# Held weight loads, idle matmuls in early gaps, and six output transposes moved from DMA to TensorE, under a newly searched order, in a recurrent-attention kernel fused with an MLP

## The chip, the cores and the metric

The kernel runs on one core of a Trainium2 chip. The metric is the time of one execution in device microseconds (us). The span of a profile, from the first to the last instruction, is 1.7 to 1.9 us shorter than that time in the profiled runs. In the profiles PE is TensorE, PEld its weight loads, DVE VectorE, ACT ScalarE, POOL GpSimd, and SP the sync engine, whose queue issues most of the transfers; a transfer has landed when its completion is recorded. An execution counts as slow when it is over 1.5% above the fastest of the same kernel. A change under 2% counts as "the same".

## The reference

The inputs are r, k and v (4 batches, 8 heads, 768 steps, 48 elements a head), w and u (8 heads x 48), and two weight matrices, 384 x 2048 and 2048 x 384.

```python
for t in range(S):                       # recurrent attention, state of 48 x 48 per head
    cur = einsum('bhd,bhe->bhde', u * k[t], v[t])
    y[t] = einsum('bhd,bhde->bhe', r[t], state + cur)
    state = w * state + einsum('bhd,bhe->bhde', k[t], v[t])
x = y as (3072 tokens, 384)
h = x @ w_in
g = where(h >= 1, h, where(h <= -1, 0, (h + 1)**2 / 4))
return g @ w_out
```

## The kernel before

The kernel cuts the 3072 tokens into 24 units of 128 steps, and two units make one block of the MLP. A unit's attention is done in parallel over its 128 steps: R and K are weighed with powers of w (products on POOL and VectorE), turned, multiplied to scores, masked, and multiplied with V; a state is carried from chunk to chunk. The unit's output x is then turned to xT, as layer 1 needs the model dimension on the partitions. In the profiles RKW is the weighed R and K before they are turned and RK after it, AT are the masked scores, Vb is V in bf16, st and T are the state's update and the state, h_p and o_p the results of the two layers, and gT is the activation. No scheduler decides the order: a list of some 1300 words, found by a search, gives the order in which all operations are issued, and each engine executes its own in that order.

```python
PE_T, PE_D, ONE = 8, 6, 2                    # units 0 to 7: turned by TensorE; the others by DMA

def load_u():
    nc.sync.dma_start(out=u_bc, in_=row_bcast(u))          # one row to 128 partitions
def load_wc():                                             # 4-byte gather, twice
    for s in range(2):
        nc.sync.dma_start(out=wc[rows[s], :], in_=w.rearrange("(p s) d -> s d p", s=2)[s])
def load(i, name):                                         # K, R or V of one unit
    nc.sync.dma_start(out=t[name, i], in_=src[b, :, c*C:(c+1)*C, :].rearrange("h s d -> s h d"))
def xp_pe(i):                                              # output turned by TensorE ...
    for kk in range(nKb):
        nc.tensor.transpose(xp[:, kk, :], t["x", i][:, kk*128:(kk+1)*128], ident)
def xp_copy(i):
    copy(("xT", i), xT[i // UB][:, i % UB], t["xp", i])
def xp_dma(i):                                             # ... or by DMA
    nc.sync.dma_start_transpose(xT[i // UB][:, i % UB], t["x", i])
def load_in(q):                                            # one quarter of w_in; w_out likewise
    nc.gpsimd.dma_start(out=w_in_sb[:, :, q*FQ:(q+1)*FQ], in_=w_in_src[:, :, q*FQ:(q+1)*FQ])
# [... weighing, scores, masks, states, layer 1 (h_p), its activation (gT), layer 2 (o_p), stores ...]
```

Of the kernel before, what the change touches and what calls it, by code (L numbers as in the profile page):

```python
# [16 lines left out]
w ld:K:0 u gi:0 ld:R:0 ln tab:K ld:K:1 tab:R Kw:0 ld:V:0 gi:1 ld:V:1 Rw:0 li:0 trp:0 gi:2 trc:0 KU1:0 at:0  # L17
KU2:0 li:1 mk:0:1 gi:3 mk:0:0 dg:0 Vb:0 ld:R:1 VD:0 st:0 Kw:1 y:0 wc x:0 li:3 KU1:1 xs:0 xp:0 Rw:1 xT:0 dec
KU2:1 trp:1 Ta:0:1 L1:0:0:0 ld:K:2 trc:1 Ta:0:0 Vb:1 dg:1 L1:0:1:0 ld:R:2 VD:1 sm:0:0:0 st:1 go:1 sm:0:1:0
Ta:1:1 at:1 li:2 Ta:1:0 L1:0:3:0 Tb:0:1 Kw:2 mk:1:0 Tb:0:0 Tb:1:1 mk:1:1 sm:0:3:0 KU1:2 Tb:1:0 ld:V:2 Rw:2  # L20
y:1 KU2:2 x:1 ld:R:3 xs:1 trp:2 go:0 dg:2 L1:0:2:0 ld:K:3 trc:2 xp:1 Vb:2 ld:V:3 sm:0:2:0 VD:2 go:3 xT:1
at:2 ld:K:4 st:2 mk:2:1 go:2 L1:0:1:1 ld:V:4 Ta:2:0 L1:0:0:1 Rw:3 sm:0:1:1 lo:0 Kw:3 Ta:2:1 Tb:2:0 L1:0:2:1
mk:2:0 sm:0:0:1 KU1:3 Tb:2:1 L1:0:3:1 sm:0:2:1 y:2 Kw:4 ld:R:4 trp:3 x:2 trc:3 KU2:3@DVE ld:R:5 dg:3 KU1:4
xp:2 L2:0:1:0 sm:0:3:1 lo:1 L2:0:0:0 Rw:4 L2:0:0:1 xT:2 L2:0:1:1 Vb:4 xs:2 at:3 KU2:4 L1:1:0:0 mk:3:1 trp:4
ld:K:5 VD:3 sm:1:0:0 L1:1:2:0 mk:3:0 Vb:3 trc:4 ld:V:5 L1:1:1:0 dg:4 sm:1:2:0 st:4 VD:4 ld:R:6 y:3 Kw:5
Ta:4:1 sm:1:1:0 L2:0:1:2 Ta:4:0 at:4 ld:K:6 x:3 st:3 Rw:5 L1:1:3:0 xs:3 KU1:5 mk:4:0 ld:V:6 L2:0:0:2
sm:1:3:0 xp:3 Ta:3:1 L2:0:1:3 KU2:5 xT:3 mk:4:1 lo:2 L2:0:0:3 trp:5 Tb:3:1 Ta:3:0 Td:4 trc:5 dg:5 L1:1:0:1
Vb:5 y:4 VD:5 sm:1:0:1 lo:3 L1:1:2:1 Kw:6 x:4 at:5 Tb:4:1 Rw:6 sm:1:2:1 L1:1:1:1 mk:5:1 xs:4 xp:4 KU1:6
mk:5:0 st:5 L1:1:3:1 ld:R:7 xT:4 Ta:5:0 sm:1:1:1 trp:6 KU2:6 Ta:5:1 ld:K:7 y:5 sm:1:3:1 L2:0:0:4 Td:5 Tb:4:0
dg:6 ld:V:7 L2:0:1:4 x:5 Vb:6 L2:0:0:5 Tb:3:0 L2:0:1:5 trc:6 ld:R:8 L2:0:1:6 xp:5 st:6 Rw:7 L2:0:0:6 Ta:6:1  # L30
xT:5 ld:K:8 L2:0:0:7 Ta:6:0 L2:0:1:7 Tb:5:1 oc:0:0 Kw:7 at:6 Tb:5:0 ld:V:8 xs:5 oc:0:1 L1:2:0 Td:6 mk:6:0
L2:1:0:0 ld:K:9 sm:2:0 L2:1:0:1 KU1:7 mk:6:1 trp:7 ld:R:9 L1:2:2 KU2:7 trc:7 L1:2:4 ld:V:9 Vb:7 sm:2:2 y:6
dg:7 Vb:8 L2:2:1:0 Tb:6:0 x:6 so:0:0 L1:2:1 Kw:8 sm:2:4 so:0:1 at:7 sm:2:1 ld:R:10 L2:1:0:2 Rw:8 mk:7:1
Tb:6:1 st:7 L1:2:3 xs:6 ld:K:11 Ta:7:1 KU1:8 xp:6 Ta:7:0 sm:2:3 L2:1:0:3 mk:7:0 L2:1:0:4 ld:V:10 xT:6 KU2:8
L1:2:5 st:8 L2:1:0:5 sm:2:5 tr:8 Td:7 y:7 dg:8 Kw:9 L2:1:0:6 x:7 Tb:7:0 L2:1:0:7 Tb:7:1 ld:R:11 L1:2:6 Rw:9
L1:2:7 sm:2:6 ld:K:12 Ta:8:1 Vb:9 L2:2:1:1 oc:1:0 sm:2:7 xp:7 KU1:9 ld:K:10 Ta:8:0 L2:2:1:2 xs:7 L2:1:1:0
L2:1:1:1 Td:8 xT:7 ld:V:11 L2:1:1:2 KU2:9 L2:1:1:3 L2:1:1:4 L2:1:1:5 tr:9 L2:1:1:6 Vb:10 dg:9 at:8 Rw:10
L1:3:3 ld:R:12 mk:8:1 L1:3:0 Kw:10 sm:3:3 mk:8:0 ld:V:12 st:9 L2:1:1:7 sm:3:0 Ta:9:1 Rw:11 L2:2:1:3 oc:1:1
L1:3:1 ld:V:13 Ta:9:0 Kw:11 y:8 sm:3:1 so:1:0 L1:3:2 x:8 Tb:8:1 tr:10 Td:9 st:10 L1:3:4 sm:3:2 KU1:11 Tb:8:0
at:9 Ta:10:0 so:1:1 sm:3:4 L2:2:1:4 KU1:10@DVE ld:R:13 L1:3:5 xs:8 mk:9:1 KU2:10 L2:2:1:5 sm:3:5 ld:K:13  # L40
L1:3:6 mk:9:0 Vb:11 L2:2:1:6 Ta:10:1 sm:3:6 xp:8 L1:3:7 KU2:11 dg:10 y:9 sm:3:7 tr:11 L2:2:1:7 Td:10 x:9
st:11 Rw:12 oc:2:1@ACT at:10 Tb:9:0 L2:2:0:0 ld:K:14 Tb:9:1 L2:2:0:1 Kw:12 dg:11 L2:2:0:2 xs:9 L2:2:0:3
ld:R:14 mk:10:0 L2:2:0:4 KU1:12 L2:2:0:5 mk:10:1 L2:2:0:6 xp:9 L2:2:0:7 KU2:12 Ta:11:1 L2:3:1:0 oc:2:0
L2:3:1:1 ld:V:14 y:10 Vb:12 Ta:11:0 L2:3:0:0 x:10 Tb:10:0 Kw:13 L2:3:0:1 so:2:1 Tb:10:1 at:11 tr:12 L2:3:1:2
Vb:13 L2:3:0:2 Rw:13 mk:11:1 L2:3:0:3 xs:10 L2:3:1:3 so:2:0 mk:11:0 L2:3:1:4 ld:K:15 Rw:14 L2:3:0:4 st:12
dg:12 L2:3:0:5 L1:4:0 xp:10 Ta:12:1 Td:11 Ta:12:0 Kw:14 y:11 sm:4:0 ld:R:15 L1:4:1 x:11 Tb:11:1 Td:12 L1:4:2
sm:4:1 ld:V:15 KU1:14 L2:3:1:5 sm:4:2 L1:4:3 tr:13 KU1:13 Tb:11:0 at:12 sm:4:3 L1:4:4 mk:12:0 KU2:13 xs:11
xp:11 L1:4:5 mk:12:1 sm:4:4 KU2:14 L2:3:0:6 ld:K:16 dg:13 sm:4:5 L2:3:1:6 L1:4:6 Vb:15@ACT Vb:14 ld:R:16
dg:14 y:12 Rw:15 sm:4:6 L1:4:7 x:12 ld:V:16 Tb:12:0 L2:3:1:7 Kw:15 sm:4:7 L2:3:0:7 st:13 tr:14 st:14
oc:3:0@ACT oc:3:1 KU1:15 at:13 Tb:12:1 Ta:13:0 xs:12 L2:4:0:0 mk:13:1 ld:K:17 L1:5:0 KU2:15 mk:13:0 L2:4:1:0  # L50
sm:5:0 xp:12 L1:5:1 Kw:16 Ta:13:1 L2:4:1:1 Ta:14:1 sm:5:1 so:3:1 L1:5:2 Ta:14:0 Rw:16 dg:15 so:3:0 y:13
sm:5:2 ld:R:17 L2:4:0:1 Td:13 x:13 L1:5:3 Td:14 Tb:13:0 ld:V:17 L2:4:1:2 Vb:16 sm:5:3 at:14 Kw:17 L2:4:0:2
tr:15 xs:13 mk:14:1 L2:4:0:3 L2:4:1:3 Tb:13:1 KU1:16@DVE L1:5:4 xp:13 mk:14:0 KU2:16 L2:4:0:4 sm:5:4
L2:4:1:4 L2:4:0:5 ld:K:18 L1:5:5 KU1:17 dg:16 y:14 ld:R:18 sm:5:5 Rw:17 L2:4:1:5 x:14 st:15 Tb:14:1 L1:5:6
ld:V:18 Tb:14:0 KU2:17 L2:4:0:6 sm:5:6 L2:4:0:7 tr:16 Ta:15:1 L1:5:7 xs:14 Vb:17 Ta:15:0 oc:4:0 at:15 Td:15
sm:5:7 L1:6:0 dg:17 xp:14 Rw:18 mk:15:1 st:16 L2:4:1:6 sm:6:0 tr:17 L2:4:1:7 mk:15:0 Kw:18 L1:6:1 oc:4:1
L2:5:1:0 sm:6:1 KU1:18 so:4:0 L2:5:1:1 Ta:16:1 y:15 Ta:16:0 ld:K:19 L2:5:0:0 Tb:15:0 x:15 Td:16 L2:5:0:1
Tb:15:1 L1:6:2 KU2:18 so:4:1 ld:R:19 L2:5:1:2 sm:6:2 L2:5:0:2 Vb:18 dg:18 L1:6:3 xs:15 ld:V:19 L2:5:1:3
sm:6:3 L1:6:4 xp:15 nsq:0 KU1:19 L2:5:1:4 at:16 ld:K:20 sm:6:4 L1:6:5 Kw:19 ns:0 L2:5:1:5 ld:R:20 sm:6:5
L2:5:0:3 mk:16:1 Rw:19 L2:5:0:4 L2:5:0:5 mk:16:0 ld:V:20 at:17 KU2:19 L1:6:6 mk:17:1 tr:18 Vb:19 y:16 sm:6:6  # L60
mk:17:0 L2:5:1:6 Kw:20 L1:6:7 Tb:16:0 x:16 ld:K:21 nsq:1 st:17 KU1:20 L1:7:0 ld:R:21 sm:6:7 y:17 Rw:20
Ta:17:1 sm:7:0 L2:5:1:7 Ta:17:0 L2:5:0:6 ld:V:21 oc:5:1 Tb:16:1 L2:5:0:7 KU2:20 xs:16 L1:7:1 oc:5:0 xp:16
L2:6:0:0 x:17 Td:17 sm:7:1 L2:6:1:0 L2:6:0:1 Vb:20 Tb:17:1 so:5:1 L1:7:2 Kw:21 Tb:17:0 so:5:0 nsq:2 L2:6:1:1
ns:1 L2:6:1:2 tr:19 Rw:21 at:18 sm:7:2 dg:19 L2:6:0:2 xs:17 L1:7:3 mk:18:0 KU1:21 xp:17 L2:6:0:3 dg:20
sm:7:3 L2:6:1:3 KU2:21 ld:K:22 mk:18:1 L2:6:0:4 L1:7:4 ns:2 Vb:21 ld:R:22 L2:6:1:4 sm:7:4 y:18 dg:21 L1:7:5
nsq:3 ld:V:22 x:18 L2:6:0:5 sm:7:5 L2:6:1:5 tr:20 L1:7:7 Kw:22 ns:3 L1:7:6 sm:7:7 ld:K:23 st:18 at:19 Rw:22
sm:7:6 Ta:18:1 L2:6:1:6 Ta:18:0 xp:18 xs:18 L2:6:0:6 mk:19:1 Td:18 L2:6:1:7 L2:6:0:7 ld:V:23 KU1:22 oc:6:1
st:19 Tb:18:1 L1:8:0 oc:6:0@ACT mk:19:0 tr:21 KU2:22 L1:8:1 Tb:18:0 Ta:19:1 sm:8:0 Ta:19:0 L2:7:0:0 sm:8:1
Vb:22 L2:7:1:0 dg:22 ld:R:23 y:19 Td:19 nsq:4 L2:7:0:1 x:19 Kw:23 at:20 so:6:1 Tb:19:1 L1:8:2 so:6:0 Tb:19:0
KU1:23 L2:7:0:2 tr:22 sm:8:2 ns:4 L2:7:0:3 L1:8:3 xs:19 mk:20:0 L1:8:4 sm:8:3 xp:19 Rw:23 mk:20:1 L2:7:0:4  # L70
sm:8:4 L2:7:1:1 L2:7:1:2 KU2:23 nsq:5 L2:7:1:3 y:20 Vb:23@ACT L2:7:1:4 dg:23 L2:7:1:5 tr:23 L1:8:5 x:20
L2:7:0:5 sm:8:5 at:21 L2:7:1:6 ns:5 L1:8:6 xs:20 L2:7:0:6 mk:21:1 sm:8:6 L2:7:1:7 xp:20 L1:8:7 nsq:6 oc:7:1
L2:7:0:7 L1:9:0 sm:8:7 oc:7:0 at:22 ns:6 sm:9:0 L1:9:1 so:7:1 mk:21:0 L2:8:1:0 sm:9:1 L2:8:0:0 so:7:0
mk:22:1 L2:8:1:1 L2:8:0:1 nsq:7 mk:22:0 y:21 L2:8:0:2 x:21 L1:9:2 L2:8:1:2 sm:9:2 L1:9:3 ns:7 L2:8:0:3
sm:9:3 L2:8:1:3 L1:9:4 xs:21 xp:21 L2:8:0:4 sm:9:4 L1:9:5 y:22 sm:9:5 L2:8:1:4 x:22 L2:8:0:5 L1:9:6 L2:8:1:5
sm:9:6 L2:8:0:6 L2:8:1:6 xs:22 at:23 L2:8:1:7 mk:23:1 L1:9:7 xp:22 oc:8:1 L2:8:0:7 sm:9:7 L1:10:0 oc:8:0
L1:10:1 mk:23:0 sm:10:0 L2:9:1:0 sm:10:1 so:8:1 L2:9:1:1 L2:9:0:0 so:8:0 y:23 L2:9:0:1 x:23 L1:10:2 L2:9:0:2
sm:10:2 L2:9:1:2 L1:10:3 xs:23 L2:9:1:3 L1:10:4 sm:10:3 xp:23 L2:9:1:4 sm:10:4 L1:10:5 L2:9:1:5 sm:10:5
L1:10:6 L2:9:1:6 sm:10:6 L2:9:1:7 L1:10:7 oc:9:1 L2:9:0:3 sm:10:7 L2:9:0:4 L2:9:0:5 L2:9:0:6 L2:9:0:7 so:9:1
# [19 lines left out]
def kernel(  # L99
# [11 lines left out]
    nc = tc.nc  # L111
# [12 lines left out]
    UB = 2  # L124
    MT = UB * C
    NB = NU // UB
    NQ = 4
    FQ, TQ = d_ff // NQ, nN // NQ
    LIM = 0.95
    PE_T, PE_D, ONE = 8, 6, 2  # L130
    mm = nc.tensor.matmul
    AX = mybir.AxisListType.X


    RING = dict(f=36, W=5, V=4, KU=3, RK=4, AT0=3, AT1=3, VD=2, x=4, g=3, o_sb=3, sq=2, a=4, h=2, o=2)

# [499 lines left out]
```

## Time and profile before

| | kernel before |
|---|---|
| time, median (range) | 191.08 us (189.82 to 193.88, 4 runs, one of them slow) |
| span of the profile | 189.3 us |
| first matmul, end of the last | 6.4, 183.6 us |
| first layer-1 matmul, first layer-2 matmul | 20.2, 34.4 us |
| TensorE work done by 30 us, by 50 us | 6.0, 22.7 us |
| TensorE time lost before 50, from 50 to 110, from 110 to 150 us | 21.0, 3.3, 5.9 us |

"Work" and "lost" are the account that the prediction introduces. Every matmul is given the spacing at which its shape follows itself in dense stretches; what passes between two starts beyond that spacing is lost. Busy time would not show this, as records of matmuls overlap (a 384-column one lasts 326 ns in the mean and starts 162 ns after the one before it). The transfers come from part 6 of the page (what, engine, count, size of each, median time from issue to landing):

```profile
R<-in_r_dram SPq DMA_DIRECT2D x24, 192.0 KB, 4.1
w_in_sb<-in_moe_w_in_dram POOLq DMA_DIRECT2D x4, 384.0 KB, 8.0
w_out_sb<-in_moe_w_out_dram POOLq DMA_DIRECT2D x4, 384.0 KB, 7.5
RK<-RKW SPq DMA_TRANSPOSE x16, 3.6
xT<-x SPq DMA_TRANSPOSE x16, 2.8
```

An output transpose by DMA lands 2.8 us after its issue in the median; the same thing on TensorE is three matmuls and a copy.

### The profile page before, as it was taken

The numbers are of one execution on the slowest core, as the hardware profiler recorded it, in microseconds if no ns is written. First come the engines' busy times: TensorE is split into PE (matmuls) and PEld (weight loads), VectorE is DVE, ScalarE is ACT, GpSimd is POOL, SyncE is SP. The second block draws the span as 40 slices with busy tenths as digits, with TensorE's granted clock in tenths as the row PEclk, the third lists the DMA queues.
The fourth block names the chain that finished last, engine by engine and source line by source line (L and its number), as shares of the span: only waits on it lengthen the run. The fifth ranks groups of instructions, "written<-read, shape, count | busy, mean of one in ns | idle before, by whom it ended". The sixth has DMA issues, their size and how long they took to land.

```text
span 189.3 us, 4565 instructions
## 1 busy us (share of the span) xinstructions
PE 161.6 (85%) x1728; PEld 121.9 (64%) x1728; DVE 115.1 (61%) x312; ACT 107.6 (57%) x227; POOL 114.7 (61%) x151
## 2 busy tenths in 40 slices
PE   0231869889999999999999998979899999999980
PEld 0121758668787687677767766657666777777750
DVE  2260898297567588985988749949749755111210
ACT  4412567869978467348766557293956545642310
POOL 8980999199799898999878387995940000000000
PEclk9999978999999999999999999999999999999997
DMA  4999999999877999879999989979994112120021
GB/s 129 202 205 168 180 202 189 187 187 194 167 182 135 204 165 211 165 184 180 157 205 180 152 206 188 193 189 155 190 226 130 27 24 83 21 83 3 23 103 57
DMA packets 106476, 28.55 MB, mean 151 GB/s; under 512 B 99408, under 2 KB 106448, under 8 KB 106448
## 3 DMA queue, kind: packets, MB, share of 16 engines
q1 hardware_dynamic: 102592, 24.95, 68.0%
q0 software_dynamic: 3712, 3.15, 10.4%
q8 instruction: 15, 0.25, 0.6%
q14 instruction: 13, 0.11, 0.2%
q10 hardware_dynamic: 144, 0.10, 0.2%
HBM read 20.84 MB, written 4.72 MB: 135 GB/s over the span
## 4 chain that ended last, share of the span: by engine, by line
PE 50%; SPq 15%; DMA 14%; POOL 9%; DVE 4%; ACT 3%; issue 3%; POOLq 0%; ACTq 0%
PE o_p L400 22%; PE h_p L373 20%; DMA R<-in_r_dram 10%; SPq L250 10%; POOL RKW L254 4%; DMA K<-in_k_dram 4%; SPq L233 3%; POOL KU L265 2%; PE A L294 2%; POOL KU L262 2%; PE y L309 1%; SPq L340 1%; PE y L306 1%; PE st L350 1%; ACT gT L384 1%
## 5 line engine op out<-in xcount | busy, mean ns | idle before, releaser
L373 PE MATMUL h_p<-xT,w_in_sb 128*128 128x256 bf16 (+1 forms) x672 | 78.3, 262 | 1.9 <-ACT gT L384 1.4
L384 ACT ACTIVATE gT<-h_p 128x512 bf16<-128x512 f32 x96 | 56.6, 595 | 39.0 <-PE h_p L373 38.0
L400 PE MATMUL o_p<-w_out_sb,gT 128*128 128x384 bf16 (+1 forms) x400 | 76.4, 320 | 0.8 <-ACT o_sb L180 0.8
L373 PEld LDWEIGHTS <-w_in_sb 128*128 128x128 bf16 x672 | 58.7, 100 | 14.3 <-issue 2.1
L400 PEld LDWEIGHTS <-gT 128*128 128x128 bf16 x400 | 36.2, 98 | 16.3 <-issue 1.0
L298 DVE TENSOR_TENSOR AT<-A,umask 128x512 bf16<-128x512 f32 x48 | 31.3, 680 | 7.3 <-PE A L294 7.2
L326 DVE SCALAR_TENSOR_TENSOR x<-Vb,dg,y 128x48 bf16<-128x48 bf16 x144 | 26.7, 257 | 9.1 <-PE y L309 8.3
L265 POOL TENSOR_TENSOR KU<-KU,R 128x384 f32<-128x384 f32 x23 | 23.9, 1043 | 12.0 <-DMA R<-in_r_dram 9.8
L254 POOL TENSOR_TENSOR RKW<-K,Winv 128x384 bf16<-128x384 f32 x24 | 24.0, 1000 | 5.1 <-DMA K<-in_k_dram 4.8
L262 POOL TENSOR_TENSOR KU<-K,u_bc 128x384 f32<-128x384 f32 x22 | 23.2, 1056 | 0.9 <-DMA K<-in_k_dram 0.9
L254 POOL TENSOR_TENSOR RKW<-R,Wpow 128x384 bf16<-128x384 f32 x18 | 18.3, 1017 | 5.4 <-DMA R<-in_r_dram 5.3
L269 DVE TENSOR_REDUCE dg<-KU 128x8 f32<-128x384 f32 x24 | 13.1, 547 | 12.2 <-POOL KU L265 12.0
L180 ACT CAST Tbd<-T 48x192 bf16<-48x192 f32 x40 | 13.9, 349 | 10.0 <-POOL T L361 5.7
L180 DVE COPY o_sb<-o_p 128x384 f32<-128x384 f32 x20 | 10.8, 552 | 14.0 <-PE o_p L400 13.7
L278 PE MATMUL tr<-ident,RKW 128*128 128x128 bf16 x64 | 6.7, 254 | 12.4 <-POOL RKW L254 6.4
L344 ACT ACTIVATE x<-x 128x384 bf16<-128x384 bf16 x24 | 12.5, 519 | 3.3 <-DVE x L326 3.0
L278 PEld LDWEIGHTS <-RKW 128*128 128x128 bf16 x64 | 5.0, 113 | 13.7 <-DVE RKW L254 6.8
L356 DVE TENSOR_TENSOR T<-T,st 48x192 f32<-48x192 f32 x32 | 11.1, 351 | 3.4 <-PE st L350 2.6
L254 DVE TENSOR_TENSOR RKW<-R,Wpow 128x384 bf16<-128x384 f32 x6 | 4.5, 751 | 13.2 <-DMA R<-in_r_dram 13.2
L180 POOL CAST Vb<-V 128x384 bf16<-128x384 f32 x22 | 11.4, 519 | 0.6 <-DMA V<-in_v_dram 0.6
L309 PE MATMUL y<-Vb,AT 128*128 128x48 bf16 x192 | 9.2, 186 | 2.1 <-DVE AT L298 2.1
L294 PE MATMUL A<-RK 48*128 48x128 bf16 x192 | 9.8, 222 | 1.1 <-ACT RK L180 1.1
(56 smaller groups left out, 120.7 us busy)
## 6 DMA issues: line engine op xcount, KB each, us to landing
K<-in_k_dram SPq DMA_DIRECT2D x24, 192.0 KB, 4.1
R<-in_r_dram SPq DMA_DIRECT2D x24, 192.0 KB, 4.1
V<-in_v_dram SPq DMA_DIRECT2D x24, 192.0 KB, 4.4
out_dram<-o_sb SPq DMA_DIRECT2D x23, 192.0 KB, 2.2
w_in_sb<-in_moe_w_in_dram POOLq DMA_DIRECT2D x4, 384.0 KB, 8.0
w_out_sb<-in_moe_w_out_dram POOLq DMA_DIRECT2D x4, 384.0 KB, 7.5
RK<-RKW SPq DMA_TRANSPOSE x16, 3.6
xT<-x SPq DMA_TRANSPOSE x16, 2.8
```

The source lines that it names most:

```text
L180: (eng.copy if eng is nc.scalar else eng.tensor_copy)(to, src)
L250: nc.sync.dma_start(out=t[name, i], in_=src[b, :, c * C : (c + 1) * C, :].rearrange("h s d -> s h d"))
L254: at_engine((name + "w", i)).tensor_mul(RKW[i % RING["W"]][:, off : off + H, 0:D], t[name, i], tab)
L262: at_engine(("KU1", i)).tensor_mul(t["KU", i], t["K", i], u3)
L265: at_engine(("KU2", i)).tensor_mul(t["KU", i], t["KU", i], t["R", i])
L269: nc.vector.reduce_sum(t["dg", i], t["KU", i], axis=AX)
L294: mm(t["A", i][s][:, p, :], KT[rows[s], p, :], RT[rows[s], p, :], start=True, stop=True)
L298: nc.vector.tensor_mul(t["AT", i, s], t["A", i][s], umask4)
L326: nc.vector.scalar_tensor_tensor(x[:, h * D : (h + 1) * D], t["Vb", i][:, h, :], t["dg", i][:, h : h + 1], t["y", i][:, h, :], op0=ALU.mul ...
L373: mm(h_p[:, f, :], w_in_sb[:, kk, (nf * n + f) * 128 : (nf * n + f + 1) * 128], xT[m][:, :, kk, :] if u_ is None else xT[m][:, u_, kk, :], ...
L384: nc.scalar.activation(g, h_p, AF.Square, bias=0.5, scale=0.5)
L400: mm(t["o", m, u, part_], t["g", m][:, f, u * C : (u + 1) * C], w_out_sb[:, f, e], start=(f == 0), stop=(f == nN - 1),)
```

## The change

The intent is to start the matrix half earlier and to unload the sync queue. Weight pieces wait for attention loads (a one-element POOL copy reads the awaited tile, and the weight transfer follows it in POOL's order). Idle matmuls against the identity fill early gaps to keep TensorE's clock up. u comes as one row and is spread by a matmul; the decay comes from eight small matmuls instead of a gather. Outputs of units 8 to 13 are turned by TensorE. The search then gave another order, with other choices of engine.

```diff
-    PE_T, PE_D, ONE = 8, 6, 2
+    PE_T, PE_X, PE_D, ONE = 8, 14, 6, 2
+    def warm(count):                              # cut: takes an output bank once, keeps it
+            for i in range(count):
+                mm(spare[0][:, d_out:], ident, ident, start=False, stop=False, skip_group_check=True)
     def load_u():
-        nc.sync.dma_start(out=u_bc, in_=row_bcast(u))
+        nc.sync.dma_start(out=u_row, in_=bass.AP(tensor=u.tensor, offset=u.offset, ap=[[0, 1], [1, H * D]]))
+    def spread_u():
+        mm(t["u"], onef, u_row, start=True, stop=True)
-    def load_wc():  ...
+    def turn_w():
+                mm(t["wp"][rows[s], p : p + 1], lw[0:1, h * D : (h + 1) * D], onef[0:1, 0:1], start=True, stop=True)
+    IN = [(0, 1, "K1"), (1, 2, "R1"), (2, 3, "V1"), (3, 4, "K2")]
+    OUT = [(0, 1, "K3"), (1, 2, "R3"), (2, 3, "V3"), (3, 4, "K4")]
+    def wait_for(j, f):
+        nc.gpsimd.tensor_copy(hold[0:1, j : j + 1], t[held(f)][0:1, 0, 0:1])
+    def load_in(z):
+        wait_for(z, f)
+        nc.gpsimd.dma_start(out=w_in_sb[:, :, a * FQ : e * FQ], ...)
-        if pe:
+        if i < PE_X:
             op(("xp", i), "PE", 0.22, (xp_pe, i), [("x", i)], d + 7, [("a", [("xT", i)])])
@@ the order (cut: all of it changes); its first words @@
-w ld:K:0 u gi:0 ld:R:0 ln tab:K ld:K:1 tab:R Kw:0 ld:V:0 gi:1 ld:V:1 Rw:0 li:0 trp:0 gi:2 ...
+w u ld:K:0 ld:K:1 ln warm*12 ub tab:K ld:R:0 Kw:0 wt uc ld:V:1 tab:R KU1:0 dec ld:R:1 gi:0 ld:V:0 Rw:0 KU2:0
+warm*41 trp:0 ld:R:2 trc:0@DVE gi:1 li:0 dg:0 warm*11 at:0 Vb:0 ...
```

In the order's words, ld is a load, gi and go are the issues of w_in and w_out pieces, trp is a unit's transposes on TensorE, at its scores, xp and xT its output's transposes and copy, L1 and L2 the layers.

## The prediction

> **What bounds the kernel now.** I read the page first (engine shares, then the forty slices), then the busy time by stretches, then the waits, then the timeline of the first 26 us and the chain that ended last. The shares and slices of the page:
>
> ```profile
> PE 161.6 (85%) x1728; PEld 121.9 (64%) x1728; DVE 115.1 (61%) x312; ACT 107.6 (57%) x227; POOL 114.7 (61%) x151
> ...
> PE   0231869889999999999999998979899999999980
> ...
> POOL 8980999199799898999878387995940000000000
> PEclk9999978999999999999999999999999999999997
> DMA  4999999999877999879999989979994112120021
> ```
>
> TensorE is nearly full after slice 8, but slices 1 to 4 are almost empty, and there is a dent between slices 23 and 30. POOL and DMA both run close to full until slice 29 (about 142 us) and then stop: the attention half feeds the matrix half until then, and after it TensorE works alone. The stretches say the same in numbers (window, its length, busy us of each engine with counts, granted clock, DMA share, GB/s):
>
> ```profile
> 0.00:26.00 26.00, 8.57 (x89) 6.59 (x89) 11.31 (x23) 9.99 (x19) 18.89 (x35) 1.00 1.04 178
> 26.00:50.00 24.00, 22.24 (x331) 18.50 (x332) 17.27 (x31) 19.04 (x42) 18.97 (x22) 0.93 1.11 190
> 50.00:110.00 60.00, 59.99 (x637) 44.78 (x635) 45.94 (x143) 39.35 (x89) 52.03 (x65) 1.00 0.95 176
> 110.00:150.00 40.00, 37.23 (x376) 26.77 (x374) 31.47 (x87) 24.56 (x52) 24.81 (x32) 1.00 0.84 170
> 150.00:184.00 34.00, 33.59 (x301) 25.31 (x299) 9.08 (x30) 14.64 (x29) 0.00 (x0) 1.00 0.15 46
> ```
>
> Busy time overlaps from one matmul to the next, so I counted TensorE's need by spacing instead. In dense places six layer-1 matmuls of 256 columns take 0.65 us and four of 384 columns take 0.65 us (chain rows), so 0.109 and 0.162 us each; the others come at 0.056 (128 columns), 0.042 (96), 0.025 (48) and about 0.030 us (score pairs). Laying each start in the trace against the spacing due after the matmul before it gives work of 146.3 us and lost time of 30.6 us. The span is then 6.4 (first matmul) + 146.3 + 30.6 + 6 (end of the last matmuls, store, check of the flag) = 189.3. The lost time lies so: 17.9 before 30 us, 3.1 from 30 to 50, 3.3 from 50 to 110, 5.9 from 110 to 150, 0.5 after. Up to 30 us only 6.0 us of work is done. The gain must come from there or from the 5.9.
>
> Why the start is empty: the waits (first) and the timeline.
>
> ```profile
> DVE RKW L254 <- DMA R<-in_r_dram: 13.2, 3, 6.1
> ...
> PE tr L278 <- DVE RKW L254: 6.1, 3, 4.6
> ```
> ```profile
> 11.05 3.58 SPq L233 DMA_DIRECT2D wc<-in_w_dram  x1
> 14.67 0.58 SPq L250 DMA_DIRECT2D K<-in_k_dram  x1
> ...
> 19.23 0.56 DVE L254 TENSOR_TENSOR RKW<-R,Wpow 128x384 bf16<-128x384 f32 x1 [6.06 <-DMA R<-in_r_dram]
> ...
> 20.14 2.60 PEld L373 LDWEIGHTS <-w_in_sb 128*128 128x128 bf16 x24
> 20.25 2.67 PE L373 MATMUL h_p<-xT,w_in_sb 128*128 128x128 bf16 x24
> ```
>
> R of unit 1 was issued at 6.2 and landed at 19.2 (issue and landing records), as the four weight pieces were in flight beside it (landed 10.7, 13.7, 16.1, 18.6). The 4-byte gather of wc held the sync queue from 9.1 to 14.7. The first layer-1 matmul therefore starts at 20.2, and at 111 ns each rather than 56, so at half clock; the clock records show full clock at 22.7, half again from 26.1 to 29.5.
>
> **What the Trainium skill says.** "TensorE: Matmul & The Clock Gate", Part 1: the array starts at half rate and is released after some 3.4 us of activity, and falls back after an idle window. The trace agrees (111 against 56 ns; 3.4 us of half clock after a gap of 1.66 us at 24.0 us). "DMA: Bandwidth & Descriptors", Issuing engines are not separate DMA queues: transfers from sync and gpsimd share the 16 engines and interleave. The trace agrees: 13 us for R of unit 1 against a median of 4.1. The same page, Rules for kernel authors: a strided last dimension makes one descriptor per element; wc shows it, as its two issues took 1.9 and 3.6 us for 0.8 KB. "TensorE: Matmul & The Clock Gate", Part 4: a TensorE transpose lands in PSUM and needs a copy after it; the trace has that copy (xT<-xp) at 0.47 us on ACT.
>
> **The change part by part.**
>
> Held weights: each weight piece is issued only after a named load has landed. Total transfer does not shrink. Packet time over 16 engines: 1.07 us for each K, R or V load (73728 packets of 192 B, 16.75 ns each, over 72 loads), 10.2 us for w_in, 9.5 for w_out. The first nine loads take 9.6, w 0.6, w_in 10.2: all landed near 2.5 + 20.4 = 23 us. But units 0 and 1 are complete at about 10 instead of 19.2, and w_in piece 0, issued after K of unit 1 and two POOL products (about 7.5), lands near 12 to 13. I expect the first layer-1 matmul near 15.5: scores of unit 0 near 11.5 (below), 1.4 for two masks, 0.3, 0.5, and 1.5 for outputs, copies and transposes. Gain there: 4 to 5 us. The w_out pieces move later (issued from about 24; now 21.0, 25.1, 26.3, 27.0), first landing near 30, last near 38, so layer 2 of block 0 begins near 30 (now 34.4).
>
> u and wc: 0.57 us of DMA (the broadcast of u) and two issues of 5.5 us on the sync queue go; a one-row product and eight one-column ones come in, about 1 to 2 us of TensorE when it is idle.
>
> Idle matmuls: 126 in the sequence, 128 columns each. Warm, 126 x 0.056 = 7.1 us; 53 of them precede the first real transpose, and there most run at half clock (0.111 each, up to 5.7 us). I choose transposes of unit 0 near 10 rather than 7.5, so some of the wait is self-made; it is hidden by the weights. The remaining 73 cost 4.1 us, nearly all in gaps. They save the half clock: half of the 2.4 us before 22.7 and of the 2.6 us busy in the cold window at 26 to 29.5, so about 2.5 us.
>
> Outputs of units 8 to 13 on TensorE: six DMA transposes go, each 1.20 us of the sync queue's issue and 384 packets x 24.9 ns / 16 = 0.6 us of DMA. Saved: 7.2 us of sync queue, 3.6 of DMA. Added: 18 matmuls x 0.056 = 1.0 us of TensorE and six copies of 0.47 (ACT) or 0.36 (DVE), off the path. From 100 to 142 us the sync queue spends 38.8 of 42 us issuing, in order, and the chain there runs through K and R landings and POOL products, so this is on the path.
>
> Order: POOL loses ten products and gains two, net -8 us of its 114.7; DVE takes about 5. In program order, the work ahead of unit 5's scores is 25.2 us (idle ones left out) against 19.5 now, and what remains after it is 126.0 against 130.2 (my spacing sums; their total is 2% above the trace's).
>
> **The sum.** By 30 us I expect 12 us of work done (now 6.0): block 0's layer 1 (5.4), half of block 1's, attention of three units (4). Loads up to R of unit 5 need 2.5 + 0.6 + 18 x 1.07 + 19.7 = 42 at one engine set, 38 at the rate that before reached (43.7 us of packet time in its first 40), so unit 5's scores come near 44 instead of 45.9. The path through it: 44 + 126.0 = 170, against 45.9 + 130.2 = 176.1. Gain 6.1. Between there and the end the old kernel lost 183.5 - 176.1 = 7.4 more. The new one should lose about the same: the earlier work asks for an earlier feed, and the freed sync queue (7.2) and POOL (8) roughly pay for that. For unit 22, 38.0 us remain after its scores in both orders; now they start at 144.9, and an end 6 us sooner needs 139, which the 7 us of sync queue just allows. So span 189.3 - 6.4 = 182.9, and with the 1.5 us between span and time, 184.4; I round to **184.2**.
>
> **The rivals.** First, the feed does not follow: the transposes of units 20 to 23 still arrive near 141, as loads wait in line on the sync queue behind transposes that wait for POOL. For: 1.0 to 1.2 us transposes of units 14 to 23 stay there, DMA share 0.84 in that stretch. Then the early gain returns as waits at 110 to 150 and the time is 187 to 190. Second, the idle matmuls and holds delay the start: POOL waits in order for K of unit 2 and for w_out's holds, so products come late, and the first layer-1 matmul is at 18 or later; time 187 to 189. Against: before 30 us the DMA, not POOL, is last. Third, the order fits so well that the 5.9 us from 110 to 150 vanish too: 179 to 181. The tail of 5.7 us after the last matmul is the same in all.
>
> **Range and chances.** The third rival sets the low end, half of the first the high end: 179.8 to 188.0. Faster by over 2% means under 187.0; I give 0.82, the same 0.16, slower 0.02.
>
> **What would show it.** Right: first layer-1 matmul at 14 to 17 us, no half clock after about 13; TensorE's work done by 30 us at 11 to 13; first layer 2 near 30; unit 5's scores at 42 to 46; fewer sync issues between 70 and 100 us, transposes of unit 23 landed by 139 (now 143.0); POOL finished by 137 (now 141). Wrong: stalls in 110 to 150 above 8 us, or layer 1 still after 18 us.

## The result

The changed kernel takes 183.34 us in the median (182.69 to 185.61, 4 runs, one of them slow), against 191.08. The ratio is 0.9605, with a 95% interval of 0.9534 to 0.9676: faster. Ratios are the mean time of one kernel's fast runs over that of the other's of the same rounds, so not quite the ratio of the medians quoted, which include the slow runs. The predicted 184.2 is 0.9 us off and the range of 179.8 to 188.0 holds the result.

The page of the changed kernel (shares, then slices of 4.5 us):

```profile
PE 168.5 (93%) x1891; PEld 129.7 (71%) x1891; DVE 120.5 (66%) x330; ACT 105.8 (58%) x225; POOL 109.0 (60%) x151
...
PE   6987686989999999999999999999999999999980
...
POOL 7797389634999797999988997932950000000000
PEclk9999999999999999999999999999999999999999
DMA  4999989999999999899999899989943022020131
```

TensorE looks busy from the first slice, but much of that is idle matmuls. The dent of slices 23 to 30 is gone, and POOL and DMA finish sooner. The stretches, with the columns as in the prediction:

```profile
0.00:26.00 26.00, 20.17 (x287) 17.10 (x288) 15.52 (x36) 11.61 (x25) 19.04 (x40) 1.00 0.97 170
26.00:50.00 24.00, 22.04 (x309) 17.38 (x307) 14.28 (x27) 14.22 (x30) 17.46 (x24) 1.00 1.10 194
50.00:110.00 60.00, 60.00 (x667) 45.53 (x663) 51.86 (x157) 41.02 (x92) 56.04 (x70) 1.00 1.00 188
110.00:150.00 40.00, 40.00 (x435) 29.82 (x433) 33.76 (x97) 28.07 (x59) 16.46 (x20) 1.00 0.66 144
```

From 110 to 150 us TensorE is busy for all of 40 us, against 37.2 before, and POOL needs 16.5 us there instead of 24.8. The start, in the timeline (start, length, engine, line, what, and in brackets the idle time before it with what ended it):

```profile
8.01 0.95 POOL L465 DMA_DIRECT2D w_in_sb<-in_moe_w_in_dram  x1
9.69 0.61 PE L306 MATMUL tr<-ident,RKW 128*128 128x128 bf16 x8
...
16.43 0.83 PE L401 MATMUL h_p<-xT,w_in_sb 128*128 128x128 bf16 x12 [0.25 <-ACT xT L182]
...
20.25 0.84 PE L401 MATMUL h_p<-xT,w_in_sb 128*128 128x128 bf16 x12 [1.78 <-DMA w_in_sb<-in_moe_w_in_dram]
```

Layer 1 starts at 16.4 us instead of 20.2. The second group then waits 1.8 us for a weight piece. R of unit 1 lands at 8.9 us instead of 19.2.

Counted as for the table above, the spans compose as follows (us):

| | before | changed |
|---|---|---|
| until the first matmul | 6.4 | 1.4 |
| real work (idle matmuls, spreading of u and decay left out) | 146.3 | 147.3 |
| idle matmuls, spreading of u, decay | 0 | 7.7 |
| lost before 50 us | 21.0 | 14.0 |
| lost from 50 to 110 us | 3.3 | 3.5 |
| lost after 110 us | 6.4 | 2.2 |
| last matmul's end and the tail | 5.9 | 5.6 |
| span | 189.3 | 181.7 |

The first, third and fourth rows together are the cost of the start: 27.3 us before and 23.1 in the changed kernel, before rounding. So the gain of 7.6 us is 4.3 at the start, 4.2 after 110 us and 0.3 in the tail, less 1.0 of added work and 0.2 in the middle. The experiments ask which parts of the change made these two.

### The profile page after: what moved, and what is told of

It reads as the page before. It is cut to its first block, busy times and chain, and to the rows that moved or that the text cites. A ratio compares the mean times of both kernels' runs of the same rounds, so it can differ in the third digit from the quotient of the medians.

```text
span 181.7 us, 4899 instructions
## 1 busy us (share of the span) xinstructions
PE 168.5 (93%) x1891; PEld 129.7 (71%) x1891; DVE 120.5 (66%) x330; ACT 105.8 (58%) x225; POOL 109.0 (60%) x151
## 4 chain that ended last, share of the span: by engine, by line
PE 77%; DMA 13%; SPq 5%; POOL 2%; issue 0%; ACT 0%
PE o_p L432 34%; PE h_p L401 31%; DMA K<-in_k_dram 7%; DMA w_out_sb<-in_moe_w_out_dram 6%; SPq L278 4%; PE A L322 4%; PE y L337 2%; PE y L334 2%; PE st L378 2%; PE xp L362 1%; POOL w_out_sb L470 1%; PE tr L306 1%; POOL RKW L282 1%; PE y L343 0%; POOL hold L460 0%
## 5 line engine op out<-in xcount | busy, mean ns | idle before, releaser
L401 PE MATMUL h_p<-xT,w_in_sb 128*128 128x256 bf16 (+1 forms) x672 | 75.1, 257 | 2.2 <-DMA w_in_sb<-in_moe_w_in_dram 1.8
L282 POOL TENSOR_TENSOR RKW<-K,Winv 128x384 bf16<-128x384 f32 x21 | 22.0, 1052 | 3.4 <-DMA K<-in_k_dram 1.9
L182 DVE COPY o_sb<-o_p 128x384 f32<-128x384 f32 (+1 forms) x20 | 10.6, 542 | 19.9 <-PE o_p L432 19.7
L293 POOL TENSOR_TENSOR KU<-KU,R 128x384 f32<-128x384 f32 x20 | 20.3, 1018 | 5.2 <-DMA R<-in_r_dram 2.5
L182 ACT CAST Tbd<-T 48x192 bf16<-48x192 f32 x40 | 13.9, 348 | 15.4 <-DVE T L386 10.3
L282 POOL TENSOR_TENSOR RKW<-R,Wpow 128x384 bf16<-128x384 f32 x14 | 14.0, 1000 | 0.2 <-DMA R<-in_r_dram 0.2
L282 DVE TENSOR_TENSOR RKW<-R,Wpow 128x384 bf16<-128x384 f32 x10 | 7.8, 782 | 8.0 <-DMA R<-in_r_dram 7.9
L389 POOL TENSOR_TENSOR T<-T,wc 128x192 f32<-128x192 f32 x16 | 9.5, 593 | 5.3 <-DVE T L384 5.3
L240 PE MATMUL w_p<-ident 128*128 128x128 bf16 x120 | 10.7, 255 | 0.0
L240 PEld LDWEIGHTS <-ident 128*128 128x128 bf16 x126 | 9.7, 117 | 0.3
L322 PEld LDWEIGHTS <-RK 48*128 48x128 bf16 x192 | 5.4, 94 | 6.0 <-issue 4.9
```

The lines of the kernel that those rows point to most:

```text
L182: (eng.copy if eng is nc.scalar else eng.tensor_copy)(to, src)
L240: mm(spare[0][:, d_out:], ident, ident, start=False, stop=False, skip_group_check=True)
L282: at_engine((name + "w", i)).tensor_mul(RKW[i % RING["W"]][:, off : off + H, 0:D], t[name, i], tab)
L293: at_engine(("KU2", i)).tensor_mul(t["KU", i], t["KU", i], t["R", i])
L322: mm(t["A", i][s][:, p, :], KT[rows[s], p, :], RT[rows[s], p, :], start=True, stop=True)
L401: mm(h_p[:, f, :], w_in_sb[:, kk, (nf * n + f) * 128 : (nf * n + f + 1) * 128], xT[m][:, :, kk, :] if u_ is None else xT[m][:, u_, kk, :], ...
```

## The experiments

All twelve kernels gave correct results. One table has the account for every run, to be used below; "a" stands for an edit of the changed kernel, "b" for an edit of the kernel before. The attempt called a_best has no row, as its profile fell in a slow run. The columns are the first layer-1 matmul, real work done by 30 and by 50 us, time lost from 50 to 110 and from 110 to 150 us, and the span, all of the profiled run in us, then the median time and the ratio to the kernel before on the same chip.

| | first L1 | by 30 | by 50 | lost 50-110 | lost 110-150 | span | median | ratio |
|---|---|---|---|---|---|---|---|---|
| before | 20.2 | 6.0 | 22.7 | 3.3 | 5.9 | 189.3 | 191.08 | 1 |
| changed | 16.4 | 9.4 | 27.1 | 3.5 | 2.0 | 181.7 | 183.34 | 0.9605 |
| after_again | 17.1 | 8.6 | 27.1 | 3.5 | 2.0 | 181.4 | 183.64 | 0.9583 |
| a_no_idle | 15.0 | 9.4 | 28.6 | 3.5 | 2.0 | 180.1 | 182.82 | 0.9503 |
| a_early_w | 25.7 | 4.7 | 20.1 | 3.5 | 2.0 | 189.1 | 191.04 | 0.9944 |
| a_xp_dma | 16.8 | 9.4 | 26.6 | 11.5 | 2.0 | 189.2 | 191.49 | 0.9951 |
| a_pool_back | 15.3 | 9.4 | 27.2 | 3.5 | 2.0 | 181.2 | 183.11 | 0.9523 |
| b_xp_pe | 19.7 | 6.3 | 23.1 | 3.4 | 2.8 | 186.8 | 188.63 | 0.9908 |
| b_hold | 15.7 | 7.8 | 22.7 | 3.5 | 5.0 | 188.1 | 190.09 | 0.9933 |
| b_idle | 19.7 | 6.1 | 23.1 | 3.4 | 6.7 | 189.7 | 191.09 | 1.0007 |
| b_hold_xp | 15.8 | 7.9 | 22.4 | 3.4 | 2.4 | 187.2 | 188.86 | 0.9873 |
| a_swap | 15.4 | 9.6 | 28.1 | 3.5 | 2.0 | 180.7 | 182.81 | 0.9607 |
| a_best2 | 14.9 | 9.6 | 28.7 | 3.5 | 2.0 | 179.9 | 182.55 | 0.9545 |

The chips differ: the kernel before took 190.7 to 192.8 us in the median of the three batches, so an edit is best compared with the others of its batch. The first batch is a_no_idle, a_early_w, a_xp_dma and a_pool_back; the second b_xp_pe, b_hold, b_idle and a_swap; the third the rest.

### Without the idle matmuls

```diff
-            warm(int(token[5:]))
             continue
```

> The changed kernel without its 126 idle matmuls, all else equal. Theory, the clock: they hold TensorE at full clock from 9.3 us on, so without them the prologue and the first layer-1 groups run at half clock until somewhere near 20 to 25 us, and half of some 4 us of early matmuls plus longer steps in the chain of unit 0 are added: 184.8 to 186. Rival, the weights set the pace: TensorE waits for pieces of w_in (20.2 us) and w_out (29 to 39 us) anyway, and the idle matmuls held back the transposes of unit 0 (data at 8.0, start at 9.7): within 0.7 us of the 183.3 of the changed kernel.

Measured: 182.82 us, ratio 0.9503, beside 0.9523 for a_pool_back in the same batch, which keeps the idle matmuls and otherwise behaves like the changed kernel. The clock theory fails: nothing is lost without them. TensorE does run at half clock, first until 16.8 us (layer-1 matmuls 107 ns apart, no clock record yet) and again from 20.2 to 23.6 us, which the clock line of its page shows in slices 4 and 5, counted from 0, as 7 and 8:

```profile
PEclk9999789999999999999999999999999999999996
```

Its work by 30 us is the same 9.4, as the weights set the pace there, and by 50 us it is even 1.5 us ahead. a_best2 below, also without idle matmuls, gets the full clock only at 22.9 us and has the shortest span of all the profiles. In the changed kernel the idle matmuls also stood in the way: unit 0's weighed R was ready at 8.0 us, and the block of 41 kept its transposes back until 9.7.

### Idle matmuls alone, in the kernel before

```diff
+warm*40 before trp:0, warm*16 before at:0, warm*24 before st:0, warm*12 before xp:0, warm*66 before trp:1
```

> The kernel before with idle matmuls alone, 158 in the gaps of its first 19 us. Theory, the clock: full clock before 12 us and no relapse at 26, so first layer-1 matmuls at 56 instead of 111 ns; 1.5 to 2.5 us less, ratio 0.987 to 0.993. Rival: the time is set by transfers (R of unit 1 at 19.2, w_out), so the faster matmuls only wait longer: ratio 0.996 to 1.004.

Measured: ratio 1.0007 (0.993 to 1.0085). The first layer 1 starts at 19.7 us as in b_xp_pe, where there are none, and 23.1 us of work are done by 50 in both. The full clock lasts from 14.2 to 24.4 us and then gives way to half clock until 31.2, so they did not prevent the relapse either; b_xp_pe gets its full clock only at 28.6 us and has done the same work by 50. The rival holds: this part brings no time that these runs can show.

### Early weights in the changed kernel

```diff
-        wait_for(z, f)                      # in load_in
-... Kw:0 ... KU1:0 ... gi:0 ... KU2:0 ... gi:1 ... gi:2 ... gi:3
+... gi:0 Kw:0 gi:1 gi:2 ... KU1:0 ... KU2:0 gi:3 ...
```

> The changed kernel with the four w_in pieces issued early, as in the kernel before (first POOL work, no hold), and w_out unheld. Theory, the holds make the start: R of unit 1 lands at 17 to 19 us instead of 8.9, the first layer 1 (which stands behind unit 1's transposes) starts near 19 to 20.5 instead of 16.4, the time is 185.5 to 187.5. Rival, the sum of transfers rules: the second unit is late, but w_in is all there at 18 instead of 22.7 and w_out unchanged, so by 32 us, where layer 2 begins, nothing is lost: 183 to 184.3.

In the kernel that ran, the holds of w_out had stayed. Measured: 191.04 us, so nearly the whole gain is gone, more than either theory expected. Layer 1 starts at 25.7 us and only 20.1 us of work are done by 50, 7.0 less than in the changed kernel. The waits of TensorE (total, times, longest), and the timeline:

```profile
PE st L359 <- POOL Vb L163: 9.1, 1, 9.1
```
```profile
19.76 0.50 POOL L163 CAST Vb<-V 128x384 bf16<-128x384 f32 x1 [8.75 <-DMA V<-in_v_dram]
20.31 0.48 PE L359 MATMUL st<-Vb,RKW 128*128 128x96 bf16 x4 [9.06 <-POOL Vb L163]
...
25.71 0.96 PE L382 MATMUL h_p<-xT,w_in_sb 128*128 128x128 bf16 x12
```

In the new order V of unit 0 is issued after R of unit 1. With the weights in flight beside it, it lands at 19.7 us instead of 9.8, and POOL and TensorE, which work in order, stand still for it. TensorE's clock is half from 15.7 to 26.0 us, during and after that stall; what this adds was not separated. From 50 us on this kernel loses exactly what the changed one loses (3.5, then 2.0), so the 7.0 us pass to the end undiminished: the span is 7.4 us longer. So in the new order the late weights are no extra: with its loads in this sequence, it depends on them.

### Held weights alone, in the kernel before

```diff
-    gi:0 ... gi:1 ... gi:2 ... gi:3 (first POOL work)
+    gi:0 after KU1:0, gi:1 after KU2:0, gi:2 after Vb:0, gi:3 after Kw:1, each behind a copy of K1, R1, V1, K2
+    ld:R:1 before ld:V:0, ld:K:2 before wc
```

> The kernel before with held w_in pieces alone (same four loads awaited; R of unit 1 and K of unit 2 issued a little earlier, w_out as it was). Theory, holding is what opens the start: R of unit 1 lands near 9 to 10 instead of 19.2, the first layer 1 starts at 15 to 17 instead of 20.2: ratio 0.975 to 0.99. Rival, the old order can't use it (the gather of wc still holds the sync queue, so K, R, V of unit 2 and later are as late as before): first layer 1 earlier, but ratio 0.992 to 1.005.

Measured: ratio 0.9933 (0.983 to 1.0035), near the edge between the two theories and not clear of no change (one of its four runs was slow). The mechanism can be read: R of unit 1 lands at 8.4 us, layer 1 starts at 15.7, and by 30 us 1.8 us more work is done than before. By 50 us nothing of it is left (22.7 in both). Two rows of its timeline show where it went:

```profile
35.99 0.40 PE L260 MATMUL tr<-ident,RKW 128*128 128x128 bf16 x4 [1.24 <-POOL RKW L236]
37.80 0.40 PE L260 MATMUL tr<-ident,RKW 128*128 128x128 bf16 x4 [1.41 <-DVE RKW L236]
```

These are unit 4's transposes. K and R of unit 4 land at 34.9 and 37.0 us, R as late as in the kernel before (37.1), as the sum of transfers is unchanged. The old order has the transposes before the layer-2 work that TensorE could do meanwhile, and so it waits. The rival is nearer, though it named the gather of wc, which in this run issued early (8.0 to 9.5 us): the wait is for unit 4's loads.

### Outputs of units 8 to 13 by DMA again

```diff
-    PE_T, PE_X, PE_D, ONE = 8, 14, 6, 2
+    PE_T, PE_X, PE_D, ONE = 8, 8, 6, 2      # and xT:8 to xT:13 taken out of the order
```

> The changed kernel with the outputs of units 8 to 13 turned by DMA again (six sync-queue transposes in the same places of the order). Theory, the sync queue feeds too late: 7.2 us of issue come back between 66 and 95 us, the transposes of unit 23 land near 141 to 143 instead of 137.3, lost TensorE time from 110 to 150 us rises from 2.0 to 4 to 6: 185.5 to 187.5. Rival, the queue has room now (33 of 42 us from 100 to 142): within 0.6 us of 183.3, or 1.0 less as 18 matmuls go.

Measured: 191.49 us, again nearly the whole gain, and at another place than expected: the loss is 11.5 us from 50 to 110 (3.5 in the changed kernel) and still 2.0 from 110 to 150. TensorE's waits, and the timeline of the longest one:

```profile
PE h_p L400 <- DMA xT<-x: 6.2, 3, 3.5
```
```profile
84.36 1.49 DVE L353 SCALAR_TENSOR_TENSOR x<-Vb,dg,y 128x48 bf16<-128x48 bf16 x8
...
87.42 2.09 SPq L367 DMA_TRANSPOSE xT<-x  x1
...
91.66 0.71 PE L400 MATMUL h_p<-xT,w_in_sb 128*128 128x256 bf16 x3 [3.54 <-DMA xT<-x]
```

x is complete at 85.85, its transpose is issued at 87.42 behind two others, and it lands at 91.6: 5.8 us, and 3.4 us of half clock follow the gap (91.8 to 95.2). In the changed kernel the transposes and the copy together take 1.0 us, as at 81 us:

```profile
81.26 0.33 PE L362 MATMUL xp<-ident,x 128*128 128x128 bf16 x3
...
81.78 0.47 ACT L182 COPY xT<-xp 128x384 bf16<-128x384 bf16 x1
```

So neither theory is right. The feed from the sync queue is not what fails first; layer 1 itself waits for the landing of xT, because the new order places it close behind x. The feed is late too (transposes of unit 23 at 147 us instead of 137), but by 110 us the 8 us are already lost, so it is more likely a result of these waits than their cause.

### Outputs of units 8 to 13 on TensorE alone, in the kernel before

```diff
-        x_done = [("xT" if i < PE_T else "xp", i) ...]
+        x_done = [("xT" if i < 14 else "xp", i) ...]      # xp and xT likewise; xT:i set behind xp:i in the order
```

> The kernel before with this part alone: outputs of units 8 to 13 turned by TensorE, copied by ACT. Theory, the freed sync queue is worth time by itself: last transposes 3 to 6 us earlier than 143.0, lost TensorE time from 110 to 150 us from 5.9 to 2 or 3: ratio 0.98 to 0.99 (187 to 189). Rival, the old order gains nothing from it (waits of the queue for POOL remain, and the copies delay ACT): ratio 0.995 to 1.01.

Measured: ratio 0.9908 (0.9838 to 0.9979). Lost time from 110 to 150 us falls from 5.9 to 2.8, and the start is unchanged, as the first theory says; 1.0 us of added work is paid. The sync queue spends 23.6 instead of 27.5 us issuing from 70 to 100 us, and the first DMA transposes of RK after 70 us are issued at 71.6 instead of 73.8. The last of them lands at 142.8, no earlier than 143.0, so that sign of the theory did not come.

How the freed queue helps is therefore argued and not shown. In the kernel before, TensorE's longest waits from 110 to 150 us are for ACT, and ACT, which works in order, had stood for a state product of POOL (first TensorE's waits in that stretch, then ACT's timeline):

```profile
PE h_p L373 <- ACT gT L384: 1.4, 2, 1.2
...
122.73 0.72 ACT L180 CAST Tbd<-T 48x192 bf16<-48x192 f32 x2 [3.22 <-POOL T L361]
```

In b_xp_pe the only wait listed there is one of 0.4 us. The loss sits in the attention chain that feeds the matrix half; that the queue's issue time is the link in it which gave way was not isolated.

### Both parts together in the old order

> The kernel before with two parts, held w_in and outputs of units 8 to 13 turned by TensorE, in the old order. Alone they gave ratios of 0.993 and 0.991. If the parts add up: 0.982 to 0.986. If the new order is what turns the earlier start into time (in the old one the start's gain was lost again between 30 and 50 us): 0.988 to 0.993, with 22.5 to 23.5 us of work done by 50 us as before. If the two parts make the whole gain once together: 0.965 to 0.975.

```diff
 b_hold
+b_xp_pe's edit: units 8 to 13 turned by TensorE, xT:i set behind xp:i in the order
```

Measured: 0.9873 (0.981 to 0.9937), between the band for mere addition and that for a start whose gain is lost; the interval covers both. The account decides for the second: 22.4 us of work by 50 us, no more than before, and 2.4 us lost from 110 to 150. The kernel keeps the late gain and not the early one. The rest, from 0.987 to 0.958, needs the new order.

### POOL's work put back

```diff
-Rw:9@DVE KU1:9@DVE KU2:11@DVE Rw:15@DVE KU2:18@DVE Kw:21@DVE Rw:21@DVE Rw:22@DVE Vb:21@ACT
+Rw:9 KU1:9 KU2:11 Rw:15 KU2:18 Kw:21 Rw:21 Rw:22 Vb:21
```

> The changed kernel with the eight products and one cast of units 9 and later that moved from POOL to other engines put back on POOL (order unchanged). Theory, POOL's load is what made the late stage wait: 8.5 us of work come back on an engine busy 56.0 of 60 us from 50 to 110; POOL ends near 139 to 142 instead of 133.9, lost time from 110 to 150 rises from 2.0 to 4 to 6: 185.5 to 188. Rival, the order and the sync queue made the gain: within 1 us of 183.3, lost time under 3.

Measured: 183.11 us, lost time 3.5 and 2.0 as in the changed kernel. Relieving POOL in the later units is worth nothing here; POOL's unit work even ends at 133.5 us, no later than the 133.9 of the changed kernel. The rival holds.

### Attempts at a better version

```diff
-warm*41 trp:0          ... L1:0:0:0 ... L1:0:2:0 ... L1:0:1:0
+warm*26 trp:0          ... L1:0:0:0 ... L1:0:1:0 ... L1:0:2:0     # a_swap
+ (no idle matmuls)     ... the same swap                          # a_best
+ a_best without wait_for in load_out                              # a_best2
```

> An attempt at a better version: the changed kernel with 26 instead of 41 idle matmuls ahead of unit 0 (its data are ready at 8.0, the transposes start at 9.7) and the second layer-1 group taken from w_in piece 1 (landed 17.8) instead of piece 2 (20.2). If early TensorE time carries to the end: 1 to 2.5 us less than the changed kernel, 181 to 182.3. If the early time is lost again waiting for w_out (29 to 39 us): within 0.5 us of 183.3.

> The changed kernel again, as the yardstick on this chip for the two attempts beside it: 182.7 to 183.8.

> The changed kernel without idle matmuls and with the second layer-1 group taken from w_in piece 1 (landed 17.8) instead of piece 2 (20.2). After 50 us every variant of the new order lost the same 5.7 us of TensorE time, so I expect time won before 50 us to reach the end one for one: the removed idle work gave 1.5 us of span, the swap up to another 1; 181.3 to 182.5, ratio to the changed kernel 0.988 to 0.995. Rival: both only remove the same wait, the arrival of w_out sets the pace until 40 us: 182.3 to 183.3.

> As a_best, and the four w_out pieces no longer held (they keep their place in POOL's order; only the wait for K of unit 3, 2.6 us in the changed kernel, is a real one). If the arrival of w_out sets the pace of 30 to 40 us: first layer 2 near 29 to 30 instead of 32, and 1 to 2 us less than a_best. If the hold protects K, R, V of units 3 and 4: these land 1 to 3 us later, scores of unit 3 and 4 are late, and the time is that of a_best or up to 1.5 us more.

a_swap took 182.81 us, below the changed kernel's 183.34 but on another chip, and its ratio of 0.9607 shows no gain. The third batch has the yardstick on the same chip with five rounds. There the changed kernel's fast runs have a mean of 183.37 us (182.11 to 183.85, 6 runs), a_best's 182.10 (181.51 to 183.23, 6 runs, and a slow one of 186.18), a_best2's 182.52 (181.76 to 183.58, 6 runs). So a_best is 1.27 us or 0.7% faster than the changed kernel, the fastest mean of its batch; two standard errors of that difference are 0.8 us. That is the size of the work gained by 50 us (1.5 us in the profile of a_no_idle). It is no "faster" by the 2% measure. Letting w_out go unheld changes nothing that these runs can resolve, as the mean of a_best2 is 0.4 us above that of a_best.

## Why the prediction was right, and where its steps were not

**What bounds the kernel** was right as to where the time lay: the gain came from the start and from the 5.9 us after 110, and from nowhere else.

**Held weights.** Right in mechanism, and b_hold and a_early_w show it from both sides. Layer 1 was expected near 15.5 and started at 16.4; w_out was expected from 30 to 38 and landed from 29.3 to 39.2. The size at the start was off: 12 us of work by 30 us were expected and 9.4 were done. Layer 2 began at 32.1 instead of 30, and the second layer-1 group waited 1.8 us for w_in's third piece, which the estimate had not placed: it gave the first piece's landing and left the others out. Unit 5's scores came at 46.8 instead of 44. By 50 us 4.4 us more work was done than before.

**Idle matmuls.** "They save ... about 2.5 us" failed. The half clock is real, but a_no_idle has it and loses nothing, and b_idle gains nothing. The sign "no half clock after about 13" came in the profile of the changed kernel but not in that of after_again, the same program, where TensorE fell to half clock from 21.6 to 25.1 us with the idle matmuls in place and had still done 27.1 us of work by 50. Two readings behind the estimate were off as well: the cold window shows 3.22 us of busy time, not 2.6, and the gap of 1.66 us before it is that of the weight loads, while the matmuls paused 1.49 us. So the trace agrees with the page that it cites on the half rate, but not on an idle window before the fall (last section). The first group's matmuls were faster only to wait for the weights. The step that the idle block would hold the first transposes until near 10 was right (9.7), and it is the one cost of this part that the profile shows; that the weights would hide it was wrong only by a little, as removing the block and the swap together gave 1.3 us.

**The six output transposes.** That the sync queue "is on the path" fits the old order only. There the relief of the queue goes with 3.1 us less lost from 110 to 150 us, by a path that stays open. In the new order what counts is the latency from x to xT, 1 us instead of up to 5.8, which the prediction did not weigh at all: it counted issue and transfer time only.

**"The new one should lose about the same"** after unit 5 is the step that failed. Unit 5's scores came at 46.8 us instead of 44, so the prediction's path through them gives 46.8 + 126.0 = 172.8 against 176.1: a gain of 3.3, not 6.1. From there to the last matmul's end at 176.3 only 3.5 us were lost, where the sum kept the old 7.4. These two errors, 2.8 and 3.9 us, have opposite signs, so the close total is partly luck. The account by time says the same: the loss after 50 us was 5.7 us instead of the old 9.7, and the variants of the new order that keep the six transposes on TensorE lose 5.7 too (a_early_w 0.3 more, after 150). The third rival, that the late loss would vanish too, came two thirds true, but the start gave less than it assumed.

**The sum's last lines** have slips of their own. Its terms give a gain of 6.1 us, not the 6.4 that is subtracted; the profiled run of the kernel before is 1.8 us longer than its span, not 1.5; and 184.4 is not 184.2 rounded. The terms as they stand give 189.3 - 6.1 + 1.8 = 185.0, 1.7 us above the result and still within the range.

**"The freed sync queue (7.2) and POOL (8) roughly pay"**: the share of POOL is refuted by a_pool_back for units 9 and later; the offloads of earlier units were not tried. What the new order itself contributes was tried only by leaving it out: b_hold_xp has 2.4 us lost after 110, near the new order's 2.0, so the late gain can be had from the transposes without the new order, and the early gain was seen only with order and holds together. The change of u and wc was not tested by itself and stays open. The 5.5 us that the prediction gave to the gather of wc was no fixed cost, though: the same two issues took 1.6 us in b_xp_pe and b_idle and 1.5 in b_hold. In b_xp_pe, whose order is the old one there, R of unit 3 was then issued at 18.5 instead of 19.3 us. So these issue times do not show the one descriptor per element of the cited page; the packets do, with 444 of four bytes between 16 and 19 us in the kernel before, for 384 elements and what else was that small.

**The rivals.** The first (the feed does not follow) did not come: RK of unit 23 landed at 137.3, POOL ended its unit work at 133.9, both earlier than asked. The second had one true part, the idle block, too small to matter.

## What to carry to other kernels

When the stretches after a point lose the same time in every variant, time won before that point reaches the end nearly one for one, and time lost as well (7.0 us by 50 us and 7.4 in the span, in a_early_w); look for the first stall there, not at shares of busy time. An order found by a search leans on the latencies that it was searched with: taking back one part of such a change (early weights, or a DMA transpose of up to 5.8 us in place of a TensorE step of 1 us) cost about as much as the whole change had gained, though the same part alone in the old order was worth 1% or less. So parts of such a change can't be valued by removal alone.

## What the Trainium skill lacked or had wrong

- "TensorE: Matmul & The Clock Gate", Part 1, gives an idle window of about 3.4 us as the cause of a fall to half clock (and, for one other kernel, short idle times between groups of matmuls, without a figure). Here a window need not be idle: the ones just before two falls had 1.71 us (before) and 1.74 us (after_again) of TensorE busy time. Nor does the busy time alone decide: windows of 2.13 to 2.30 us (changed kernel) were followed by no fall, but one of only 1.63 us (a_pool_back) was not followed by one either. The windows are laid by each trace's own clock records, whose changes lie multiples of 3.41 us apart. Each row is a stretch of one window; the first two are of the kernel before, the next two of after_again, then one of the changed kernel and two of a_pool_back, and the number after the five busy times is the granted clock:

```profile
22.68:26.09 3.41, 1.71 (x29) 1.25 (x26) 3.35 (x5) 2.59 (x6) 3.33 (x5) 1.00 1.25 182
26.09:29.50 3.41, 3.22 (x33) 2.84 (x35) 3.12 (x4) 2.26 (x5) 3.40 (x5) 0.50 1.25 202
```
```profile
18.20:21.60 3.40, 1.74 (x32) 1.38 (x30) 2.88 (x6) 0.40 (x1) 2.07 (x4) 1.00 1.24 206
21.60:25.10 3.50, 3.50 (x43) 3.04 (x40) 1.44 (x4) 2.56 (x4) 1.45 (x3) 0.51 0.74 143
```
```profile
16.10:19.50 3.40, 2.13 (x36) 1.66 (x33) 2.01 (x5) 1.79 (x3) 2.40 (x3) 1.00 1.24 204
```
```profile
18.65:22.07 3.42, 1.63 (x30) 1.63 (x31) 1.58 (x4) 0.75 (x2) 0.10 (x1) 1.00 1.16 197
22.07:25.48 3.41, 2.93 (x61) 2.51 (x59) 2.98 (x8) 3.36 (x9) 2.33 (x5) 1.00 0.51 99
```

- The same page, Why this matters for your kernels, advises against idle gaps of more than about 3 us between bursts of matmuls, to hold the clock. It does not say that this brings no time where TensorE waits for transfers anyway, as it did here: without the 126 idle matmuls the ratio was 0.9503, with them 0.9523 in the same batch; in a_no_idle TensorE waits 2.7 us for a piece of w_in.
- "DMA: Bandwidth & Descriptors", DMA Transpose (X-bar), gives no latency for one small transpose from SBUF to SBUF. Here a 128 x 384 one took 1.2 us of the sync queue to issue and a median of 2.8 us (2.3 to 4.8 in the kernel before) from issue to landing, beside 1.0 us for TensorE with its copy.
